# Features 256 to 639 of the first tokens: DMA transposes in place of TensorE turns

## The chip, the cores and the metric

The kernel runs on one core of a Trainium2 chip. A core has TensorE (matrix multiplication into PSUM), VectorE, ScalarE and GpSimd (elementwise work) and SyncE, which here only issues DMAs; each follows its own queue of instructions and waits for the others through semaphores. The metric is the time of one execution on the device in microseconds, the median of several runs. Data is bf16; PSUM holds f32.

## The reference

The input x holds 2048 tokens of 640 features. Two branches see the same x and a gate of each token mixes them:

```python
g = sigmoid((x * gate_w).sum(-1, keepdims=True))
# branch A: a state space layer with 640 complex states
dt = exp(log_dt); Lam_bar = exp(dt * Lam)
B_bar = ((Lam_bar - 1.0) / Lam)[:, None] * Bmat
Bu = einsum("bld,pd->blp", x, B_bar)
for t in range(L):                 # L = 2048
    h = Lam_bar * h + Bu[:, t, :]
a = 2.0 * einsum("blp,dp->bld", hseq, Cmat).real + x * Dskip
# branch B: a dense layer of two matrices, hidden size 1728
b = gelu(x @ w1 + b1) @ w2 + b2
return g * a + (1 - g) * b
```

## The kernel before, in words

**Tiling.** The tokens are cut into four chunks of 512 (c = 0 to 3), a chunk into four blocks of 128 tokens (a = 0 to 3), the 640 features into five slices of 128 (kd = 0 to 4), and the 1728 hidden columns into 14 groups (kf), 13 of 128 and one of 64. The first dense layer (`ff1`, `ff1_mm`, L264) and the product with B (`ssm`, L540) need x with the features on the partitions: the tile `xT[c]`, 128 partitions by 5 slices by 512 tokens. The skip term x * Dskip (`seed`, L576) needs x with the tokens on the partitions: the tile `xn[c]`. The second dense layer is `fin_b` (L605), the product of the states with C is `fin_a` (L653).

**Where xT comes from.** For chunks 1, 2 and 3 a DMA transpose reads x from DRAM and writes xT (L175, L184, L185). For chunk 0, x is loaded into `xn[0]`, block by block, and TensorE turns each block and slice by a matmul against an identity (`turn`, L232, with its matmul on L233). The result stands in PSUM, from where `turned` (L236) copies it to xT, with VectorE (L240) or ScalarE (L242). `turn_first` does this for slices 0 and 1 of a block, `turn_rest` for slices 2, 3 and 4, three matmuls and one copy of 384 columns a block. The constant KA = 2 marks the border between the two.

**The loads.** `load_x0` loads a part of `xn[0]`, `load_w1a` a slice of the first 768 columns of w1 (`w1a`, groups kf 0 to 5). The next 512 columns are `w1b`, the last 448 are `w1c`, with one more column that a copy fills with gate_w (L399). `rows` loads a parameter vector as rows of `prmA` (log_dt, Lambda_im, Lambda_re) or `prmB` (gate_w, b1), and a matmul against the identity turns these into columns (L371, L396). The loads stand at L138 to L186, nearly all in SyncE's queue; ScalarE's queue issues w1a[0], w1a[1] and one load of x0. SyncE issues in the order of the text. Semaphores are given to DMAs in turn, and a DMA that is given one already in use waits until the earlier DMA has landed.

**The order of work around the change.** From L188 on, the order of the instructions of TensorE, VectorE and ScalarE is the order of the text. After nine warming matmuls (L230), six banks of PSUM collect the groups kf 0 to 5 of chunk 0. `strip(kd, t0, t1, ...)` adds slice kd for tokens t0 to t1 to all six, and `part(kd, a)` is the strip of one block. Matmuls of slices 0 and 1 stand between the turns of the four blocks (L359 to L368), then come slices 2 and 4 and, with the last slice 3, the loop over kf at L394. Between them stand the small operations that make the step sizes, angles and decay (`dt16`, `dtl`, `thp_c`, `r_c`, `u`, `kk`, `red`, `ab`), the two sines on ScalarE (L391, L393), and the turned columns of prmB at kf = 3. Six GELUs follow on ScalarE, then w1b and w1c, then `ssm(0)`. While these run, VectorE doubles the tables of cosine and sine (L416 to L436), and then it scans.

**The later order** is written out at L686 to L710: ssm and ff1 of a chunk, and fin_b and fin_a some steps later. `let_out` and `dve_now` put VectorE's operations in between by planned times. Two buffers of `xn` are used in turn, so `load_xn(3)` (L701) stands after the last use of xn[1].

Of the kernel before, what the change touches and what calls it, by code (L numbers as in the profile page):

```python
# [12 lines left out]
BF16 = mybir.dt.bfloat16  # L13
# [3 lines left out]
P = 128  # L17
T = 2048
D = 640
F = 1728  # L20
CH = 512
NCH = T // CH
KD = D // P
KS = D // P
# [3 lines left out]
TPC = CH // P  # L28
H = TPC // 2
HT = H * P  # L30
# [11 lines left out]
def kernel(  # L42
# [19 lines left out]
    nc = tc.nc  # L62
    x2d = A_x.flatten_outer_dims()
# [3 lines left out]
    const = ctx.enter_context(tc.tile_pool(name="const", bufs=1))  # L67
# [7 lines left out]
    def bank(dtype=F32):  # L75
        return ps.tile([P, CH * 4 // (4 if dtype == F32 else 2)], dtype, name="bank")


    cut1 = FA * P
    FB = FA + 4  # L80
    cut2 = FB * P
    n1c = F - cut2 + 1
    xT = [const.tile([P, KD, CH], BF16, name=f"xT{c}") for c in range(NCH)]
    w1a = [const.tile([P, cut1], BF16, name=f"w1a_{kd}") for kd in range(3)]
    w1a34 = const.tile([P, 2, cut1], BF16, name="w1a34")
    w1a += [w1a34[:, j, :] for j in range(2)]
    w1b = [const.tile([P, cut2 - cut1], BF16, name=f"w1b_{kd}") for kd in range(KD)]
    w1c = [const.tile([P, n1c], BF16, name=f"w1c_{kd}") for kd in range(KD)]
    w2_sb = const.tile([P, KF - 1, D], BF16, name="w2_sb")
    BT_re, BT_im = ([const.tile([P, KD, n * P], BF16, name=f"BT_{ri}{n}") for n in (KSA, KS - KSA)] for ri in ("re", "im"))  # L90
    CT_re = const.tile([P, KS, D], BF16, name="CT_re")
# [4 lines left out]
    prmA = const.tile([P, P], BF16, name="prmA")  # L96
    NB = KS + KF - 1
    prmB = const.tile([P, P], BF16, name="prmB")
# [21 lines left out]
    def load_xn(c, a0=0, a1=TPC, queue=None):  # L120
        if a0 == 0:
            xn[c] = xnp.tile([P, TPC, D], BF16, name="xn")
        r0 = c * CH + a0 * P
        (queue or nc.sync).dma_start(out=xn[c][:, a0:a1, :], in_=x2d[r0:r0 + (a1 - a0) * P, :].rearrange("(a p) d -> p a d", p=P))

    def load_w1a(queue, kd):
        queue.dma_start(out=w1a[kd][:], in_=B_w1[kd * P:(kd + 1) * P, 0:cut1])

    def rows(queue, dst, v):
        queue.dma_start(out=dst, in_=v.rearrange("(j p) -> j p", p=P))  # L130

    KA = 2
    xn[0] = xnp.tile([P, TPC, D], BF16, name="xn")

    def load_x0(queue, a0, a1, d0, d1):
        queue.dma_start(out=xn[0][:, a0:a1, d0:d1], in_=x2d[a0 * P:a1 * P, d0:d1].rearrange("(a p) d -> p a d", p=P))
# [3 lines left out]
    load_x0(nc.sync, 1, 2, 0, KA * P)  # L140
    load_w1a(nc.scalar, 1)
    load_x0(nc.sync, 2, 3, 0, KA * P)
    load_x0(nc.scalar, 0, H, KA * P, D)
    load_x0(nc.sync, 3, 4, 0, KA * P)
    load_w1a(nc.sync, 2)
    nc.vector.memset(prmA[:], 0.0)
    nc.vector.memset(prmB[:], 0.0)
    warm = const.tile([P, 1], F32, name="warm")
    nc.scalar.activation(out=warm[:], in_=nc.const_aps.tensor(1.0, [P, 1], BF16), func=ACT.Exp)
    rows(nc.sync, prmA[0:KS, :], A_log_dt)  # L150
    rows(nc.sync, prmA[KS:2 * KS, :], A_Lambda_im)
    rows(nc.sync, prmA[2 * KS:3 * KS, :], A_Lambda_re)
    load_x0(nc.sync, H, TPC, KA * P, D)
    nc.sync.dma_start(out=w1a34[:], in_=B_w1[3 * P:KD * P, 0:cut1].rearrange("(k p) f -> p k f", p=P))
    rows(nc.sync, prmB[KS:NB, :], B_b1[0:(KF - 1) * P])
    rows(nc.sync, prmB[0:KS, :], gate_w)
    for kd in range(KD):
        nc.sync.dma_start(out=w1b[kd][:], in_=B_w1[kd * P:(kd + 1) * P, cut1:cut2])
    for kd in range(KD):
        nc.sync.dma_start(out=w1c[kd][:, 0:F - cut2], in_=B_w1[kd * P:(kd + 1) * P, cut2:F])  # L160
    make_identity(nc, ident[:])
    HC = CH // 8
    tfi = work.tile([P, HC], I32, name="e")
# [15 lines left out]
        nc.sync.dma_start(out=w2_sb[:, k0:k1, :], in_=B_w2[k0 * P:k1 * P, :].rearrange("(kf p) d -> p kf d", p=P))  # L179
    for h in range(2):  # L180
        nc.sync.dma_start(out=w2l[h * F_LAST:(h + 1) * F_LAST, :], in_=B_w2[(KF - 1) * P:F, :])
    nc.sync.dma_start(out=b2bc[:], in_=B_b2.rearrange("(o d) -> o d", o=1).to_broadcast([P, D]))
    nc.sync.dma_start(out=Dbc[:], in_=A_Dskip.rearrange("(o d) -> o d", o=1).to_broadcast([P, D]))
    nc.sync.dma_start_transpose(out=xT[2][:], in_=x2d[2 * CH:3 * CH, :])  # L184
# [32 lines left out]
    def pe(cols):  # L217
        ck.pe += cols / 2400.0 + 0.002
# [9 lines left out]
    pA = bank()  # L228
# [3 lines left out]
    def turn(p, col, a, kd):  # L232
        nc.tensor.matmul(p[:, col:col + P], lhsT=xn[0][:, a, kd * P:(kd + 1) * P], rhs=ident[:], start=True, stop=True,  # L233
                         skip_group_check=True)

    def turned(engine, p, col, a, k0, k1):  # L236
        dst = xT[0][:, k0:k1, a * P:(a + 1) * P]
        src = p[:, col:col + (k1 - k0) * P].rearrange("p (k t) -> p k t", t=P)
        if engine is nc.vector:
            nc.vector.tensor_copy(out=dst, in_=src)  # L240
        else:
            nc.scalar.activation(out=dst, in_=src, func=ACT.Identity)  # L242

    def turn_first(a, other):
        t = bank()
        turn(t, 0, a, 0)
        turned(nc.vector, t, 0, a, 0, 1)
        turn(other, a * P, a, 1)
        turned(nc.scalar, other, a * P, a, 1, 2)

    turn_first(0, pA)

    def col(name, dtype=F32, n=KS):
# [10 lines left out]
    def ff1_mm(p, c, kf, kd, t0=0, t1=CH, first=None, last=KD - 1):  # L264
        w, f0 = (w1a, 0) if kf < FA else (w1b, FA) if kf < FB else (w1c, FB)
        w = w[kd][:, (kf - f0) * P:(kf - f0 + 1) * P]
        nc.tensor.matmul(p[:, t0:t1], lhsT=w, rhs=xT[c][:, kd, t0:t1],  # L267
                         start=(kd == 0) if first is None else first, stop=(kd == last), skip_group_check=first is not None)
        pe(t1 - t0)
# [53 lines left out]
    banks = [bank() for _ in range(FA)]  # L323

    def strip(kd, t0, t1, first, f0=0, f1=FA):
        for kf in range(f0, f1):
            ff1_mm(banks[kf], 0, kf, kd, t0, t1, first, 3)

    def turn_rest(a, t, *parts):
        for k in range(KA, KD):  # L330
            turn(t, (k - KA) * P, a, k)
        for engine, k0, k1 in parts:
            turned(engine, t, (k0 - KA) * P, a, k0, k1)

    HB = CH // 2

    def scratch(i):
# [16 lines left out]
    def part(kd, a):  # L354
        strip(kd, a * P, (a + 1) * P, kd == 0)
# [10 lines left out]
    turn_first(3, pA)  # L366
    part(0, 2)
    part(1, 2)  # L368
    turn_rest(0, pA, (nc.scalar, KA, KD))
    pP = bank()  # L370
    nc.tensor.matmul(pP[:, 0:3 * KS], lhsT=prmA[:], rhs=ident[:, 0:3 * KS], start=True, stop=True, skip_group_check=True)  # L371
    nc.vector.tensor_copy(out=colA[:], in_=pP[:, 0:3 * KS])
    nc.scalar.activation(out=dt16[:], in_=ldt_c, func=ACT.Exp)
    nc.vector.tensor_scalar(out=limp[:], in0=lim_c, scalar1=INV_2PI, scalar2=None, op0=ALU.mult)
    part(0, 3)
    turn_rest(1, bank(), (nc.vector, KA, KD))
    nc.vector.tensor_tensor(out=dtl[:], in0=dt16[:], in1=lre_c, op=ALU.mult)
    nc.vector.tensor_tensor(out=thp_c[:], in0=dt16[:], in1=limp[:], op=ALU.mult)
    nc.scalar.activation(out=r_c[:], in_=dtl[:], func=ACT.Exp)
    nc.vector.tensor_tensor(out=u, in0=tf[:].rearrange("p (o i) -> p o i", o=1).to_broadcast([P, KS, NP]), in1=over(thp_c[:], NP), op=ALU.mult)  # L380
    part(1, 3)
    part(2, 0)
    part(2, 1)
    turn_rest(2, pA, (nc.scalar, KA, KD))
    turn_rest(3, bank(), (nc.vector, KA, KD))
    nc.vector.tensor_copy(out=kk[:], in_=u)
    nc.vector.tensor_tensor(out=red, in0=u, in1=kk[:], op=ALU.subtract)
    strip(KD - 1, 0, HT, False)
    part(2, 2)
    part(2, 3)  # L390
    nc.scalar.activation(out=FSC[:, 0:KS, 0:NP], in_=red, func=ACT.Sin, scale=TWO_PI_M)  # L391
    nc.vector.scalar_tensor_tensor(out=ab, in0=red, scalar=-1.0, in1=red, op0=ALU.mult, op1=ALU.max)
    nc.scalar.activation(out=FSC[:, KS:2 * KS, 0:NP], in_=ab, func=ACT.Sin, scale=-TWO_PI_M, bias=halfpi[:])  # L393
    for kf in range(FA):  # L394
        if kf == 3:
            nc.tensor.matmul(pA[:, 0:NB], lhsT=prmB[:], rhs=ident[:, 0:NB], start=True, stop=True, skip_group_check=True)  # L396
            nc.vector.tensor_copy(out=colB[:], in_=pA[:, 0:NB])
            for j in range(KD):
                nc.vector.tensor_copy(out=w1c[j][:, n1c - 1:n1c], in_=pA[:, j:j + 1])  # L399
        for kd in (4, 3):  # L400
            ff1_mm(banks[kf], 0, kf, kd, HT if kd == 4 else 0, CH, False, 3)
    for kf in range(FA):
        ff1_act(banks[kf], 0, kf)
    two_banks = [bank(), bank()]
# [24 lines left out]
    for ks in range(KS):  # L429
        for dst, X, xs, Y in ((TCOS, FS, nsH, FC), (TSIN, FC, sH, FS)):  # L430
            t = work.tile([P, HB], F32, name="g")
# [108 lines left out]
    def ssm(c, at={}):  # L540
        hs[c] = hsp.tile([P, 2 * KS, CH], BF16, name="hs")
        for ks in range(KS):
            if ks in at:
                at[ks]()
            bu = work.tile([P, 2, CH], BF16, name="bu", bufs=8)
            for ri, BT in enumerate((BT_re, BT_im)):
                p = bank()
                for kd in range(KD):
                    nc.tensor.matmul(p[:], lhsT=BT[ks >= KSA][:, kd, (ks % KSA if ks < KSA else ks - KSA) * P:][:, 0:P], rhs=xT[c][:, kd, :],  # L549
                                     start=(kd == 0), stop=(kd == KD - 1))  # L550
                    pe(CH)
                nc.scalar.activation(out=bu[:, ri, :], in_=p[:], func=ACT.Identity)  # L552
                act(0.6)
            scan_ops(c, ks, bu, ck.act)
            if c == 0 and ks == 0:
                later(0, 1.6, factors)
            let_out(ck.pe)
# [140 lines left out]
    ssm(2, {KS - 1: lambda: first_banks(1)})  # L698
    fin_b(1, seeds(1))
    fin_a(1)  # L700
    load_xn(3)  # L701
    ssm(3)
    gel_tile(3)
    ff1(3, 0, {KF - 3: lambda: first_banks(2)})
# [36 lines left out]
```

## Time and profile before

| | |
|---|---|
| median of three runs | 215.61 us (215.58 to 215.92) |
| the profiled execution, its own time | 215.9 us |
| its span, first to last instruction | 214.1 us |
| TensorE busy | 210.6 us, 98% of the span |
| VectorE, ScalarE busy | 189.1 us (88%), 102.7 us (48%) |
| granted TensorE clock | 1.000 |
| DMA moved | 15.84 MB |

The profile is one execution. The span runs from the first to the last instruction; the rest of the execution's own time lies around it. Busy time counts the instructions of an engine, not its waits. A TensorE matmul's end is modelled, so a wait of TensorE is better seen in the distance between the starts of two matmuls. The chain of work goes back from the last instruction to whatever released it, step by step. A DMA is shown twice: by the time that its queue took to issue it, and by the time from its issue to its landing. PE is TensorE, DVE is VectorE, ACT is ScalarE, and SPq and ACTq are the DMA queues of SyncE and ScalarE.

### The profile page before, as it was taken

The page shows a single profiled execution, that of the slowest core. Times are in us where ns is not written, and L with a number is a line of the kernel's source. Part 1 is how long each engine was busy: PE and PEld are TensorE (multiplying, and loading weights), DVE is VectorE, ACT ScalarE, POOL GpSimd, SP SyncE. Part 2 cuts the span into 40 slices and gives each one's busy share as a digit, 9 for nine tenths or more (in the row PEclk, how much of TensorE's full clock was granted, in tenths as well). Part 3 has the DMA queues.
Part 4 walks back from the last instruction along what each step waited for, and adds up shares of the span by engine and source line. Part 5 has one row for each costly group of instructions (what it writes and reads, how often), then busy time and mean ns, then how long its engine had stood idle before and what let it go on. Part 6 is the DMA issues. An engine that isn't in the chain of part 4 may idle for free.

```text
span 214.1 us, 3607 instructions
## 1 busy us (share of the span) xinstructions
PE 210.6 (98%) x1413; PEld 127.4 (59%) x1413; DVE 189.1 (88%) x387; ACT 102.7 (48%) x185; POOL 1.0 (0%) x13
## 2 busy tenths in 40 slices
PE   8999999999999999999999999999999999999994
PEld 5955444454475644775457777444457687676773
DVE  1589999999998999999999999999999999993153
ACT  3499856675759579203573210455683422305100
POOL 1000000000000000000000000000000000000000
PEclk9999999999999999999999999999999999999999
DMA  6869999999000000042000005100000000100011
GB/s 191 232 147 202 207 183 287 324 211 186 0 0 0 3 0 0 17 136 109 0 3 0 0 0 183 65 0 2 3 0 14 3 0 31 61 34 0 0 66 61
DMA packets 31571, 15.84 MB, mean 74 GB/s; under 512 B 22978, under 2 KB 31554, under 8 KB 31554
## 3 DMA queue, kind: packets, MB, share of 16 engines
q1 hardware_dynamic: 30850, 14.99, 29.2%
q10 hardware_dynamic: 704, 0.62, 0.9%
q8 instruction: 11, 0.18, 0.3%
q14 instruction: 6, 0.05, 0.1%
HBM read 7.48 MB, written 2.62 MB: 47 GB/s over the span
## 4 chain that ended last, share of the span: by engine, by line
PE 98%; DVE 0%; issue 0%
PE bank L267 27%; PE bank L608 27%; PE bank L667 20%; PE bank L549 20%; PE bank L230 1%; PE bank L624 1%; PE bank L293 1%; PE bank L233 1%; DVE ot L672 0%; PE bank L358 0%; PE bank L283 0%; PE bank L396 0%; PE bank L371 0%
## 5 line engine op out<-in xcount | busy, mean ns | idle before, releaser
L608 PE MATMUL bank<-w_sb,gel 128*128 128x384 bf16 (+1 forms) x416 | 57.9, 299 | 0.0
L608 PEld LDWEIGHTS <-gel 128*128 128x128 bf16 x416 | 40.3, 98 | 17.0 <-issue 0.8
L552 ACT ACTIVATE bu<-bank 128x512 bf16<-128x512 f32 x40 | 23.6, 597 | 37.3 <-PE bank L549 37.3
L272 ACT ACTIVATE gel<-bank,colB 128x512 bf16<-128x512 f32 x52 | 33.7, 693 | 10.4 <-PE bank L267 10.1
L667 PEld LDWEIGHTS <-hs 128*128 128x128 bf16 x330 | 31.7, 98 | 11.6
L503 DVE TENSOR_TENSOR_SCAN g<-r_c,carry,v 128x512 bf16<-128x512 f32 x30 | 37.2, 1268 | 0.0
L616 ACT ACTIVATE gb<-bank,gcol 128x384 f32<-128x384 f32 (+1 forms) x32 | 15.1, 526 | 32.9 <-PE bank L608 16.4
L267 PE MATMUL bank<-xT,w1a 128*128 128x512 bf16 (+2 forms) x180 | 28.6, 315 | 0.0
L667 PE MATMUL bank<-CT_re,hs 128*128 128x320 bf16 (+2 forms) x165 | 27.1, 295 | 0.0
L667 PE MATMUL bank<-CT_im,hs 128*128 128x320 bf16 (+2 forms) x165 | 27.1, 295 | 0.0
L672 DVE SCALAR_TENSOR_TENSOR ot<-bank,gcol,gb 128x320 bf16<-128x320 f32 (+2 forms) x33 | 17.4, 531 | 9.6 <-PE bank L667 8.2
L549 PE MATMUL bank<-xT,BT_re 128*128 128x512 bf16 x100 | 24.8, 379 | 0.0
L549 PE MATMUL bank<-xT,BT_im 128*128 128x512 bf16 x100 | 24.8, 379 | 0.0
L267 PEld LDWEIGHTS <-w1a 128*128 128x128 bf16 x180 | 15.5, 102 | 11.3
L267 PE MATMUL bank<-xT,w1b 128*128 128x512 bf16 x80 | 17.9, 379 | 0.0
L549 PEld LDWEIGHTS <-BT_im 128*128 128x128 bf16 x100 | 9.8, 98 | 11.8
L582 DVE TENSOR_TENSOR bank<-xn,Dbc 128x320 f32<-128x320 bf16 (+2 forms) x33 | 14.5, 480 | 2.1 <-ACT gb L616 2.1
L549 PEld LDWEIGHTS <-BT_re 128*128 128x128 bf16 x100 | 9.6, 98 | 11.0
L484 DVE TENSOR_TENSOR v<-wa,wb 128x512 bf16<-128x512 bf16 x40 | 15.2, 421 | 0.6
L597 ACT ACTIVATE bank<-b2bc 128x384 f32<-128x384 bf16 (+1 forms) x24 | 11.7, 529 | 7.6 <-DVE ot L672 7.6
L484 DVE TENSOR_TENSOR wa<-TCOS,g 128x1024 bf16<-128x1024 bf16 x20 | 13.7, 684 | 0.1
L267 PE MATMUL bank<-xT,w1c 128*128 128x512 bf16 x60 | 13.7, 379 | 0.0
(99 smaller groups left out, 166.1 us busy)
## 6 DMA issues: line engine op xcount, KB each, us to landing
out_dram<-ot SPq DMA_DIRECT2D x15, 160.0 KB, 1.8
w_sb<-in_B_w_dram SPq DMA_DIRECT2D x1, 2080.0 KB
xn<-in_A_x_dram SPq DMA_DIRECT2D x3, 640.0 KB
w1b<-in_B_w_dram SPq DMA_DIRECT2D x5, 128.0 KB, 3.6
w1c<-in_B_w_dram SPq DMA_DIRECT2D x5, 112.0 KB, 3.2
w1a<-in_B_w_dram ACTq DMA_DIRECT2D x2, 192.0 KB, 3.0
w1a<-in_B_w_dram SPq DMA_DIRECT2D x1, 384.0 KB, 3.7
xn<-in_A_x_dram SPq DMA_DIRECT2D x4, 64.0 KB, 3.6
```

The source lines that it names most:

```text
L267: nc.tensor.matmul(p[:, t0:t1], lhsT=w, rhs=xT[c][:, kd, t0:t1], start=(kd == 0) if first is None else first, stop=(kd == last), skip_grou ...
L272: nc.scalar.activation(out=gel[c][:, kf, :], in_=p[:, :], func=ACT.Gelu_apprx_tanh, bias=b1_c[:, kf:kf + 1])
L484: nc.vector.tensor_tensor(out=o, in0=a, in1=b, op=op)
L503: nc.vector.tensor_tensor_scan(s["g"][:, ri, :], r_c[:, ks:ks + 1].to_broadcast([P, CH]), s["v"][:, ri, :], init, ALU.mult, ALU.add)
L549: nc.tensor.matmul(p[:], lhsT=BT[ks >= KSA][:, kd, (ks % KSA if ks < KSA else ks - KSA) * P:][:, 0:P], rhs=xT[c][:, kd, :], start=(kd == 0 ...
L552: nc.scalar.activation(out=bu[:, ri, :], in_=p[:], func=ACT.Identity)
L582: dve_now(ck.pe, 0.45, lambda: nc.vector.tensor_tensor(out=p[:, 0:d1 - d0], in0=xn[c][:, a, d0:d1], in1=Dbc[:, d0:d1], op=ALU.mult))
L597: nc.scalar.activation(out=v, in_=src, func=ACT.Identity)
L608: nc.tensor.matmul(p[:, col:col + d1 - d0], lhsT=gel[c][:, kf, a * P:(a + 1) * P], rhs=w2_sb[:, kf, d0:d1], start=False, stop=False, skip_ ...
L616: nc.scalar.activation(out=gbs[ti][:, d0:d1], in_=p[:, col:col + d1 - d0], func=ACT.Identity, scale=gcol[:, 1, ti:ti + 1])
L667: nc.tensor.matmul(p[:, 0:d1 - d0], lhsT=hs[c][:, j, lo:lo + P], rhs=CT[:, j % KS, d0:d1], start=False, stop=(j == 2 * KS - 1), skip_group ...
L672: nc.vector.scalar_tensor_tensor(out=ot[:, d0:d1], in0=p[:, 0:d1 - d0], scalar=gcol[:, 0, ti:ti + 1], in1=gbs[ti][:, d0:d1], op0=ALU.mult, ...
```

## The change

Slices 2, 3 and 4 (features 256 to 639) of chunk 0 no longer come from TensorE. Two DMA transposes in SyncE's queue, each for two blocks (256 tokens by 384 features), write them to xT[0]. `turn_rest` is gone with its twelve matmuls and four copies. `xn[0]` needs the same features for the skip term only and gets them by one load behind w2. The strips of slices 2 and 4 are cut at other places. Beside that:

- log_dt, Lambda_im and Lambda_re are issued by ScalarE's queue;
- ScalarE's load of x0 and SyncE's second one are gone from the start;
- w1a[3] and w1a[4] are two loads, 4 ahead of 3, instead of one, and w1c is two loads instead of five;
- the second copy of block 0 is VectorE's instead of ScalarE's;
- xn[3] is loaded in two halves.

```diff
-    w1a = [const.tile([P, cut1], BF16, name=f"w1a_{kd}") for kd in range(3)]
-    w1a34 = const.tile([P, 2, cut1], BF16, name="w1a34")
-    w1a += [w1a34[:, j, :] for j in range(2)]
+    w1a = [const.tile([P, cut1], BF16, name=f"w1a_{kd}") for kd in range(KD)]
...
-    w1c = [const.tile([P, n1c], BF16, name=f"w1c_{kd}") for kd in range(KD)]
+    w1c_lo = const.tile([P, 3, n1c], BF16, name="w1c_lo")
+    w1c_hi = const.tile([P, 2, n1c], BF16, name="w1c_hi")
+    w1c = [w1c_lo[:, j, :] for j in range(3)] + [w1c_hi[:, j, :] for j in range(2)]
...
     load_x0(nc.sync, 2, 3, 0, KA * P)
-    load_x0(nc.scalar, 0, H, KA * P, D)
+    nc.vector.memset(prmA[:], 0.0)
+    nc.vector.memset(prmB[:], 0.0)
+    rows(nc.scalar, prmA[0:KS, :], A_log_dt)
     load_x0(nc.sync, 3, 4, 0, KA * P)
     load_w1a(nc.sync, 2)
-    nc.vector.memset(prmA[:], 0.0)
-    nc.vector.memset(prmB[:], 0.0)
...
-    rows(nc.sync, prmA[0:KS, :], A_log_dt)
-    rows(nc.sync, prmA[KS:2 * KS, :], A_Lambda_im)
-    rows(nc.sync, prmA[2 * KS:3 * KS, :], A_Lambda_re)
-    load_x0(nc.sync, H, TPC, KA * P, D)
-    nc.sync.dma_start(out=w1a34[:], in_=B_w1[3 * P:KD * P, 0:cut1].rearrange("(k p) f -> p k f", p=P))
+    for a in range(0, TPC, H):
+        nc.sync.dma_start_transpose(out=xT[0][:, KA:KD, a * P:(a + H) * P], in_=x2d[a * P:(a + H) * P, KA * P:D])
+    rows(nc.scalar, prmA[KS:2 * KS, :], A_Lambda_im)
+    rows(nc.scalar, prmA[2 * KS:3 * KS, :], A_Lambda_re)
+    load_w1a(nc.sync, 4)
+    load_w1a(nc.sync, 3)
...
-    for kd in range(KD):
-        nc.sync.dma_start(out=w1c[kd][:, 0:F - cut2], in_=B_w1[kd * P:(kd + 1) * P, cut2:F])
+    for t, k0, k1 in ((w1c_lo, 0, 3), (w1c_hi, 3, KD)):
+        nc.sync.dma_start(out=t[:, :, 0:F - cut2], in_=B_w1[k0 * P:k1 * P, cut2:F].rearrange("(k p) f -> p k f", p=P))
...
         nc.sync.dma_start(out=w2l[h * F_LAST:(h + 1) * F_LAST, :], in_=B_w2[(KF - 1) * P:F, :])
+    load_x0(nc.sync, 0, TPC, KA * P, D)
...
-        turned(nc.scalar, other, a * P, a, 1, 2)
+        turned(nc.scalar if a else nc.vector, other, a * P, a, 1, 2)
...
-    turn_rest(0, pA, (nc.scalar, KA, KD))
...
     part(0, 3)
-    turn_rest(1, bank(), (nc.vector, KA, KD))
...
     part(1, 3)
-    part(2, 0)
-    part(2, 1)
-    turn_rest(2, pA, (nc.scalar, KA, KD))
-    turn_rest(3, bank(), (nc.vector, KA, KD))
+    strip(2, 0, HT, False)
     nc.vector.tensor_copy(out=kk[:], in_=u)
     nc.vector.tensor_tensor(out=red, in0=u, in1=kk[:], op=ALU.subtract)
-    strip(KD - 1, 0, HT, False)
-    part(2, 2)
-    part(2, 3)
+    strip(2, HT, CH, False)
+    strip(4, 0, CH, False)
...
-        for kd in (4, 3):
-            ff1_mm(banks[kf], 0, kf, kd, HT if kd == 4 else 0, CH, False, 3)
+        ff1_mm(banks[kf], 0, kf, 3, 0, CH, False, 3)
...
-    load_xn(3)
+    load_xn(3, 0, H)
+    load_xn(3, H, TPC)
```

More of the change, by code (lines that the diff above doesn't have):

```diff
@@ L327, in strip @@
             ff1_mm(banks[kf], 0, kf, kd, t0, t1, first, 3)
[L329 to L333, printed above, removed]
     HB = CH // 2
```

## The prediction

> **What bounds the kernel.** I read the page first: how busy each engine is, and the chain of work that ended last.
>
> ```profile
> span 214.1 us, 3607 instructions
> ...
> PE 210.6 (98%) x1413; PEld 127.4 (59%) x1413; DVE 189.1 (88%) x387; ACT 102.7 (48%) x185; POOL 1.0 (0%) x13
> ...
> PE 98%; DVE 0%; issue 0%
> ```
>
> The end is set by TensorE alone: the chain runs through its matmuls from 0.77 us to the last store, and no other engine holds 1% of it. Whatever shortens TensorE's queue ends the kernel earlier, as long as nothing makes TensorE wait instead. So I read the same chain in order of time where the change works (start us, us, what):
>
> ```profile
> 7.39 0.17 PE bank L233 x3
> 7.56 0.01 PE bank L371
> 7.57 0.35 PE bank L267 x6
> 7.92 0.27 PE bank L233 x3
> 8.19 1.14 PE bank L267 x18
> 9.33 0.34 PE bank L233 x6
> 9.66 2.30 PE bank L267 x24
> ```
>
> The L233 pieces are the twelve turns (3, 3 and 6). At these places 128-column matmuls start every 0.056 us, so twelve are worth 0.67 us; they hold 0.78 because the fourth waited 0.10 us (a start 0.157 after the one before it) for a bank that VectorE was still reading. The 18 matmuls at 8.19 should take 18 x 0.056 = 1.00 and take 1.14: the 13th waits 0.14 us for VectorE's 0.56 us copy (L240) of a turned block.
>
> Then what DMA does meanwhile: the DMA list (issue to landing, us), SyncE's waits, and the windows (last figures: DMA share, GB/s).
>
> ```profile
> xT<-in_A_x_dram SPq DMA_TRANSPOSE x3, 5.9
> BT_re<-in_A_B_re_dram SPq DMA_TRANSPOSE x2, 5.2
> BT_im<-in_A_B_im_dram SPq DMA_TRANSPOSE x2, 5.3
> ```
>
> ```profile
> SPq L130 <- DMA w1a<-in_B_w_dram: 0.4, 1, 0.4
> SPq L154 <- DMA xn<-in_A_x_dram: 0.3, 1, 0.3
> ```
>
> ```profile
> 4.00:5.00 1.00, 1.00 (x12) 1.00 (x11) 0.29 (x1) 0.29 (x2) 0.00 (x0) 1.00 1.05 322
> 5.00:6.00 1.00, 1.00 (x12) 1.00 (x11) 0.23 (x1) 0.12 (x1) 0.00 (x0) 1.00 0.58 146
> ...
> 16.00:22.00 6.00, 6.00 (x47) 3.12 (x46) 5.79 (x11) 5.99 (x13) 0.00 (x0) 1.00 1.16 199
> ```
>
> Transposes take over 5 us to land here, though they are larger (256x640 and 512x640) than the new ones. SyncE's waits show a limit: each DMA of the load block reuses the semaphore of the DMA eight places before it and isn't issued until that has landed. The DMA engines are full from 2 to 5 us and half idle from 5 to 6.
>
> [...] the trace agrees (0.107 us until 5.9 us, 0.056 after), so the turns are all in the cheap stretch. [...] the four 320 KB B transposes land at 18.03, 20.11, 22.04 and 23.97 us (semaphore records), about 2.0 us each or 164 GB/s, so I use 2.0. [...]
>
> **The change part by part.**
>
> Twelve turns leave TensorE: 12 x 0.056 = 0.67. The bank wait and the copy wait were made by turned blocks, so they go too: 0.10 + 0.14. Strips of 256 and 512 columns (0.109 and 0.216 us) replace pairs of narrower matmuls: 24 x 0.056 = 1.34 becomes 12 x 0.109 = 1.31, and 12 x 0.109 becomes 6 x 0.216, 0.01 less. The gain on the chain is 0.95 us if all data is there.
>
> Two copies leave VectorE (0.56 each) and two ScalarE (0.49 each); one 128x128 copy (0.28 to 0.29) moves to VectorE, which ends it near 4.2, before TensorE reads it at 4.67. None of these is on the chain. The dependent work must follow, and does: without the copies VectorE's dtl moves from 8.70 to about 8.0, the sine from 11.3 to about 10, and the first GELU waits only for the b1 column, 0.9 earlier with TensorE. VectorE has the least cover later: it writes the last pieces of the first chunk's hs at 86.1 and 86.4, and TensorE reads them from 87.3 and 88.0. A TensorE 0.95 us earlier still finds them, and VectorE's own chain starts earlier too (its colB copy waits for TensorE's L396).
>
> The first x columns of the four blocks keep their loads. The 192 KB load on ScalarE's queue and its twin on SyncE's (384 KB) leave the start and come back as one load behind w2, near 33 us: about 1.3 us more in front of b2bc, the turned x of chunks 2 and 3, xn and the first gelL transpose. gelL lands at 53.6 and is read at 64.5; b2bc lands at 43.2 and is used near 55. Hidden.
>
> The parameter rows now go through ScalarE's queue. log_dt is issued at 1.66 in the place of the load. Lambda_im and Lambda_re wait for the third and fourth DMAs (landed 3.85 and 4.15), so ScalarE issues them by 4.5 at 0.3 each, before its first turned block is ready at 4.70. They took up to 2.9 us to land on SyncE's queue, so 7.2 at worst; TensorE wants them at 7.23. Taken: no wait.
>
> Transposes: SyncE ends the w1a load at 3.02. The first transpose is about the ninth to eleventh DMA, so it waits for a landing between 3.4 and 4.15: issued 3.5 to 4.2. Issue costs 1.45 us for ten 128x128 blocks (BT_re), 0.9 for six, so the second goes at 4.4 to 5.1. The first B transpose moved its first packet 1.3 us after issue: 5.0 to 5.4, when the w1a data ahead has drained. Time to landing, bounded: gelL (two blocks, SBUF to SBUF) took 2.3 from issue, BT_re 4.74 with nothing transposing ahead. Six blocks on the line between give 3.5; landing 7.0 to 7.7. The second follows by 6/10 of 2.0 = 1.2: 8.2 to 8.9. Low bound for both 2.3 from issue, high bound 5.2.
>
> TensorE wants the first at 7.93 (7.40 - 0.17 for the first three turns, 0.03 for L371, 12 x 0.056), the second 6 x 0.109 later at 8.58, w1a[4] at 9.24, w1a[3] 6 x 0.216 later at 10.5, prmB at 11.2. w1a[4] is issued near 6 and lands about 0.4 behind the second transpose, 9.0; w1a[3] 0.6 later. So the second transpose is the one at the edge: I take 8.6 with half a microsecond either way: between no stall and 0.5, and 0.2 as the value. Both ends stay for the range: none, or 10.2 - 8.6 = 1.6.
>
> Behind them: the first w1b load now waits for the first transpose's landing and the second for the second's, so w1b is issued at 7.7 to 10.7 instead of 6.7 to 9.0. TensorE reads w1b[0] from 11.9 and w1b[4] from 13.6, and loads take about 3 us: cover at least 1.0 us. w1c in two DMAs instead of five saves three issues of 0.43 us, so the B transposes are issued no later than before (13.3); their first read is at 21.05 with 3.0 us to spare. The split load of xn[3] adds one issue of 0.6 us near 134 us, 50 us before its use.
>
> Sum: 214.1 - 0.95 + 0.2 = 213.35 of span. The profiled execution took 215.9 in all, 1.8 around its span, and the median is 215.61. Against the median: 215.6 - 0.75, about **214.9 us**.
>
> **Rivals.**
> - A, on time: the second transpose lands by 9.0, and the stall is at most 0.4. 214.5 to 215.1. The half-idle DMA stretch at 5 to 6 us speaks for it.
> - B, somewhat late: it lands at 9.0 to 10.0, or w1a[4] behind it at 9.6 to 10.6. The stall takes 0.4 to 1.4 and the time is 215.0 to 216.0, mostly no change.
> - C, late, the slower side: a transpose takes 5.2 us whatever its size. Issued at 5.0, the second lands at 10.2 or later, TensorE stands 1.6 us or more at the second strip, and all weights behind it are late as well: 216.1 to 217. It decides from a landing at 10.0 (8.58 + 0.95 + 0.43), since each microsecond there costs one. For it: the fixed-looking 5.2 and 5.3; against it: 2.3 for gelL, and that these rows include queueing behind the transpose before.
> - D, ScalarE's queue: if the two rows get the slots of later loads (5.2 to 6.3 us), ScalarE stands in front of its second turned block, TensorE waits for it near 5.5 and for the rows at 7.2: 215.5 to 217. The order of issue before gives no sign of it.
> - E, the turns go but the time comes back at hs near 86 us: 215.6. Against it: the cover worked out above.
>
> **Chances.** A 0.58, B 0.18, C 0.14, D 0.06, E 0.04. Faster by over 0.2% (0.43 us, about what can be told from no change here): A and a third of B, 0.64. Within: most of the rest of B, and E, 0.15. Slower: C, D and the tail of B, 0.21. The likeliest case's own range is 214.5 to 215.1; to hold 8 in 10 the range goes up through B to the edge of C, 214.5 to 216.1.
>
> **What would show it.** Right: L233 eight times only, none after 6.7 us, TensorE's first w1b matmul near 11.9 to 12.1 (12.80 before), the rest of the chain shifted by the same amount. Late transposes: a start-to-start gap over 0.11 us at the first matmul on w1a[2] with 256 columns, or on w1a[4]. D: ScalarE's second L242 later than 4.7. E: w1b near 12 but the L667 group of chunk 0 at its old 86.98. I would be wrong mostly through the landing time of a 256x384 transpose, which no row here shows.

## The result: slower, by what the merged w1c tiles do

| | before | after |
|---|---|---|
| median | 215.60 us (215.09 to 215.92, four runs) | 220.82 us (220.55 to 221.81, four runs) |
| the profiled execution's own time | 215.9 us | 221.1 us |
| its span | 214.1 us | 219.3 us |
| first matmul on w1b starts | 12.80 us | 12.12 us |
| second matmul on w1b starts | 13.02 us | 16.50 us |
| last matmul ends | 211.35 us | 216.53 us |

The ratio of after to before is 1.0253, with the 95% interval [1.0214, 1.0292]. The forecast was 214.9 us; it was wrong in sign, and 220.82 us lies outside its range. In after every line number has moved: the first dense layer's matmul is L269, the copies of the gate columns are L389, the transposes L151.

The page of after still shows TensorE at 96% of the span. It is the chain that differs: 7% of it is now DMA and SyncE's queue, and the row of the granted clock has one slice that isn't full (the fourth, which begins at 16.4 us).

```profile
span 219.3 us, 3528 instructions
...
PE 211.2 (96%) x1372; PEld 126.3 (58%) x1383; DVE 188.6 (86%) x386; ACT 102.7 (47%) x182; POOL 1.0 (0%) x13
...
PEclk9996999999999999999999999999999999999999
...
PE 91%; DMA 4%; SPq 3%; issue 1%; DVE 0%
```

The chain of after in order of time (start us, us, what) says where it leaves TensorE. Before 16.5 us it doesn't run through TensorE's matmuls, but through SyncE's issues of the two transposes and of the weights behind them, up to the second w1c load:

```profile
3.62 1.33 SPq L151
5.00 1.27 SPq L151
...
10.52 0.43 SPq L161
...
10.99 5.20 DMA w1c_hi<-in_B_w_dram
...
16.21 0.24 DVE w1c_hi L389 x2
...
16.50 7.04 PE bank L269 x24
```

What releases that chain is five copies of one column. In the kernel before, VectorE's timeline (start us, us, engine, line, operation, tiles; in brackets the idle time ahead and what ended it) has them straight behind the copy of the parameter columns:

```profile
12.10 0.18 DVE L397 COPY colB<-bank 128x18 f32<-128x18 f32 x1 [0.49 <-PE bank L396]
12.20 0.41 DVE L399 CAST w1c<-bank 128x1 bf16<-128x1 f32 x5
```

The same view of after:

```profile
11.68 0.18 DVE L387 COPY colB<-bank 128x18 f32<-128x18 f32 x1 [1.15 <-PE bank L386]
15.58 0.29 DVE L389 CAST w1c_lo<-bank 128x1 bf16<-128x1 f32 x3 [3.72 <-DMA w1c_lo<-in_B_w_dram]
16.21 0.23 DVE L389 CAST w1c_hi<-bank 128x1 bf16<-128x1 f32 x2 [0.34 <-DMA w1c_hi<-in_B_w_dram]
```

Each of these copies writes gate_w into the last column of a w1c slice. In before each slice is a tile of its own, the load fills the columns ahead of the last one, and the copy ran at 12.2 us while the five loads landed between 13.2 and 14.4: nothing waited. In after three slices share a tile, and two share another. The list of changes names the two loads; the two tiles stand only in the diff. The columns of all but a tile's last slice now lie between pieces that one load writes, and the copies wait until the whole load has landed, 15.56 and 16.19 us. No byte is written by both; that the order comes from the columns lying inside the load's range is an inference.

And TensorE waits for the copies, because they read the bank pA: six of the eight banks still hold groups, and the second of `two_banks` takes over pA's. TensorE's timeline of after shows one matmul on w1b into the other bank, and then nothing:

```profile
11.48 0.81 PE L269 MATMUL bank<-xT,w1a 128*128 128x512 bf16 x3
12.12 0.38 PE L269 MATMUL bank<-xT,w1b 128*128 128x512 bf16 x1
16.50 3.80 PE L269 MATMUL bank<-xT,w1b 128*128 128x512 bf16 x9 [4.00 <-DVE w1c_hi L389]
```

From the start at 12.12 to the one at 16.50 there are 4.38 us, where 0.216 is usual: 4.16 us are lost. In before the same place held twenty matmuls in one go (12.80 to 17.12).

The third part of the loss is in the windows of after (window, then busy us and instructions of PE, PEld, DVE, ACT and POOL, then the granted clock, DMA share, GB/s):

```profile
12.00:16.00 4.00, 0.50 (x3) 0.01 (x1) 0.29 (x3) 3.99 (x7) 0.00 (x0) 1.00 0.99 199
...
17.00:18.00 1.00, 1.00 (x4) 0.34 (x3) 0.96 (x3) 0.00 (x0) 0.00 (x0) 0.50 1.16 260
18.00:19.00 1.00, 1.00 (x3) 0.30 (x2) 0.96 (x3) 0.00 (x0) 0.00 (x0) 0.50 0.63 123
...
20.00:21.00 1.00, 1.00 (x6) 0.41 (x5) 1.00 (x2) 0.88 (x2) 0.00 (x0) 1.00 1.17 222
```

When TensorE restarts, its granted clock is 0.50 ("cold" below, "warm" being the full clock): 512-column matmuls start every 0.427 us until 19.9 us, then every 0.216 again. That costs 1.70 us over what those starts take warm. So: 0.68 gained up to the first w1b matmul, 4.16 lost to the wait, 1.70 lost to the cold clock, together +5.18 us. The last matmul ends 216.53 - 211.35 = 5.18 later, so the three terms are the whole.

### The profile page after: what moved, and what is told of

Same layout as the page of the kernel before. It is cut to its first block, busy times and chain, and to the rows that moved or that the text cites. A ratio compares the mean times of both kernels' runs of the same rounds, so it can differ in the third digit from the quotient of the medians.

```text
span 219.3 us, 3528 instructions
## 1 busy us (share of the span) xinstructions
PE 211.2 (96%) x1372; PEld 126.3 (58%) x1383; DVE 188.6 (86%) x386; ACT 102.7 (47%) x182; POOL 1.0 (0%) x13
## 3 DMA queue, kind: packets, MB, share of 16 engines
HBM read 7.48 MB, written 2.62 MB: 46 GB/s over the span
## 4 chain that ended last, share of the span: by engine, by line
PE 91%; DMA 4%; SPq 3%; issue 1%; DVE 0%
PE bank L597 26%; PE bank L269 23%; PE bank L656 20%; PE bank L538 20%; DMA w1c_hi<-in_B_w_dram 2%; DMA w1a<-in_B_w_dram 1%; SPq L151 1%; PE bank L613 1%; PE bank L295 1%; SPq L159 1%; SPq L127 0%; SPq L130 0%; SPq L161 0%; DVE ot L661 0%; DVE w1c_hi L389 0%
## 5 line engine op out<-in xcount | busy, mean ns | idle before, releaser
L274 ACT ACTIVATE gel<-bank,colB 128x512 bf16<-128x512 f32 x52 | 34.6, 686 | 17.1 <-PE bank L269 16.8
L269 PE MATMUL bank<-xT,w1a 128*128 128x512 bf16 (+2 forms) x158 | 27.8, 332 | 0.2
L269 PE MATMUL bank<-xT,w1b 128*128 128x512 bf16 x80 | 19.8, 405 | 4.0 <-DVE w1c_hi L389 4.0
L269 PEld LDWEIGHTS <-w1a 128*128 128x128 bf16 x162 | 14.7, 103 | 11.8
L269 PEld LDWEIGHTS <-w1b 128*128 128x128 bf16 x80 | 8.2, 103 | 15.0 <-DVE w1c_hi L389 4.5
```

What stands on the lines that cost most here:

```text
L274: nc.scalar.activation(out=gel[c][:, kf, :], in_=p[:, :], func=ACT.Gelu_apprx_tanh, bias=b1_c[:, kf:kf + 1])
```

## The experiments

All were timed beside the kernel before on the same chip (1 to 4, 5 to 8 and 9 apart, so that kernels of different groups compare by the ratio). "End" is the end of the last matmul in one profiled execution (before: 211.35). The timed runs of before alone reach from 214.94 to 216.56 us, so ends that differ by half a microsecond tell what happened in two executions, not what is usual.

| kernel | end us | span us | median us, and of before beside it | ratio, 95% interval |
|---|---|---|---|---|
| 1 after, w1c in five | 211.39 | 214.4 | 216.35, 215.93 | 1.0022 [1.0011, 1.0034] |
| 2 before, w1c in two | 213.21 | 216.1 | 218.94, 215.93 | 1.0158 [1.0104, 1.0212] |
| 3 after, gate columns by GpSimd | 211.74 | 214.5 | 216.42, 215.93 | 1.0026 [1.0015, 1.0037] |
| 4 after, the wait filled | 214.97 | 217.7 | 219.61, 215.93 | 1.0178 [1.0149, 1.0206] |
| 5 kernel 1, three ot buffers | 210.80 | 213.8 | 215.93, 215.89 | 1.0007 [0.9996, 1.0019] |
| 6 before, three ot buffers | 211.30 | 214.0 | 215.78, 215.89 | 0.9999 [0.9987, 1.0010] |
| 7 kernel 1, 30 small matmuls more | 210.84 | 213.9 | 215.82, 215.89 | 1.0012 [0.9996, 1.0028] |
| 8 kernel 5, w1b in two, rows read later | 210.46 | 213.2 | 215.36, 215.89 | 0.9987 [0.9974, 1.0000] |
| 9 before, rows on ScalarE's queue | 211.24 | 214.0 | 215.76, 215.91 | 0.9996 [0.9981, 1.0011] |

**Kernels 1 and 2: undo the merging alone, do it alone.** The first asks whether the rest of the change is worth anything; the second whether merging w1c hurts without the transposes. The edit of kernel 1 against after (kernel 2 has the same lines the other way round, in before):

```diff
-    w1c_lo = const.tile([P, 3, n1c], BF16, name="w1c_lo")
-    w1c_hi = const.tile([P, 2, n1c], BF16, name="w1c_hi")
-    w1c = [w1c_lo[:, j, :] for j in range(3)] + [w1c_hi[:, j, :] for j in range(2)]
+    w1c = [const.tile([P, n1c], BF16, name=f"w1c_{kd}") for kd in range(KD)]
...
-    for t, k0, k1 in ((w1c_lo, 0, 3), (w1c_hi, 3, KD)):
-        nc.sync.dma_start(out=t[:, :, 0:F - cut2], in_=B_w1[k0 * P:k1 * P, cut2:F].rearrange("(k p) f -> p k f", p=P))
+    for kd in range(KD):
+        nc.sync.dma_start(out=w1c[kd][:, 0:F - cut2], in_=B_w1[kd * P:(kd + 1) * P, cut2:F])
```

> The changed kernel with w1c in five tiles and five loads again, as before the change; all else of the change stays. Tile theory (the five gate_w column copies now wait for the merged loads of w1c, because those loads and the columns share a tile; TensorE waits behind them for the bank that they read, and its clock goes cold): VectorE copies the columns right after colB, near 11.9 us, no wait of TensorE at its second w1b matmul, and the gain of the transposes that the trace after already shows at its first w1b matmul (12.12 against 12.80) stays: 0.6 to 0.7 us under the kernel before, ratio 0.997. Rival (the transposes push w1b and w1c back in SyncE's queue, and TensorE waits for data): the w1c loads are issued later still, with five issues, and the time stays at 220 us or above, ratio 1.02 or more.

> The kernel before with w1c alone in two tiles and two loads, and nothing else of the change. Tile theory: the copies of the gate_w columns wait for the merged loads, which land near 14 us here since nothing delays their issue (9.0 and 9.5 us), so TensorE's second w1b matmul starts near 14.3 instead of 13.0: 1.3 us slower, or 2.5 to 3 if the clock goes cold as well; 217 to 218.5 us. Rival (the transposes are the cost): no wait appears, two issues instead of five help or do nothing, 215.3 to 215.8 us.

Kernel 1's TensorE reads w1b[0] at 12.20 and never stands for L387, its copies of the gate columns, which VectorE makes at once: its end is 5.14 us earlier than after's.

```profile
11.86 0.41 DVE L387 CAST w1c<-bank 128x1 bf16<-128x1 f32 x5
...
12.20 1.89 PE L267 MATMUL bank<-xT,w1b 128*128 128x512 bf16 x8
14.26 2.76 PE L267 MATMUL bank<-xT,w1b 128*128 128x512 bf16 x12 [0.17 <-DMA w1b<-in_B_w_dram]
```

Kernel 2, which keeps all twelve turns, has the wait of after in small. Its timeline of TensorE:

```profile
12.73 0.38 PE L269 MATMUL bank<-xT,w1b 128*128 128x512 bf16 x1
14.88 4.26 PE L269 MATMUL bank<-xT,w1b 128*128 128x512 bf16 x19 [1.77 <-DVE w1c_hi L401]
```

It loses 1.93 us there (2.149 from start to start), and its end is 1.86 later than before's. The wait is shorter than in after because the loads stand earlier in SyncE's queue (issued at 8.63 and 9.12, not at 10.52 and 10.99, with no transposes ahead) while TensorE comes later (12.73, not 12.12). So merging and transposes each add to the 4.16. The clock stayed warm in this profile (mean granted clock 1.000), 2.15 us lying between the two starts. The four timed runs took 217.93, 217.97, 219.91 and 221.07; the profiled one is the first. The mean granted clock on record is 1.000 and 0.998 for the two short ones and 0.990 and 0.991 for the two long ones, after's being 0.992 with its 3.4 us at half clock. So the two long ones probably had a cold stretch as well; no trace shows what they waited for, or how long.

So the merging is the cause, from both sides. Both edits change the tiles and the loads together; five loads into the two shared tiles, which would tell one from the other, were not run. But kernel 1 isn't faster than before either, though a ratio of 0.997 was expected of it: 0.6 us of gain at w1b are gone by the end. Kernels 5 to 7 follow that up.

**Kernel 3: keep the merged tiles, break the chain at the bank.** VectorE copies the five columns from PSUM to a small tile, and GpSimd copies them from there into w1c.

```diff
+            gw = const.tile([P, KD], F32, name="gw")
+            nc.vector.tensor_copy(out=gw[:], in_=pA[:, 0:KD])
             for j in range(KD):
-                nc.vector.tensor_copy(out=w1c[j][:, n1c - 1:n1c], in_=pA[:, j:j + 1])
+                nc.gpsimd.tensor_copy(out=w1c[j][:, n1c - 1:n1c], in_=gw[:, j:j + 1])
```

> The changed kernel with its merged w1c; VectorE copies the five gate columns from PSUM into a small tile of its own at once, and GpSimd copies them from there into w1c. Tile theory: GpSimd waits for the loads of w1c in place of VectorE, the bank is free near 12 us, TensorE doesn't wait, and the time is that of the first of these kernels, 214.9 us within 0.2. Rival: as slow as the changed kernel, 220 to 221 us.

The wait for the load is still there, on an engine that nobody needs then. Its timeline, with TensorE, VectorE and GpSimd:

```profile
11.96 0.15 DVE L389 COPY gw<-bank 128x5 f32<-128x5 f32 x1
...
12.30 4.60 PE L269 MATMUL bank<-xT,w1b 128*128 128x512 bf16 x20
...
15.14 1.69 POOL L391 CAST w1c_lo<-gw 128x1 bf16<-128x1 f32 x3 [13.54 <-DMA w1c_lo<-in_B_w_dram]
```

All twenty w1b matmuls run in one go. So it isn't the load's lateness as such that costs 4 us: it is the reading of a PSUM bank that TensorE needs, in an instruction that also waits for a load. The time is that of kernel 1 (1.0026 and 1.0022), and not the 214.9 us expected.

**Kernel 4: the same wait, but TensorE kept busy.** Nineteen matmuls of constants into the first of the two banks fill the time until the copies; their result is overwritten. It asks what the cold clock costs by itself.

```diff
     two_banks = [bank(), bank()]
+    for _ in range(19):
+        nc.tensor.matmul(two_banks[0][:, 0:512], lhsT=ones(P), rhs=ones(512), start=True, stop=True)
```

> The changed kernel with 19 matmuls of 512 columns on constants put in ahead of the first w1b matmul, 19 x 0.216 = 4.1 us of work without use that writes the same bank as the first w1b group and is overwritten by it. If 1.7 of the 5.2 us are TensorE's cold clock after 4 us of standing still (eight starts 0.427 us apart instead of 0.216), the fill keeps it warm and the kernel is 1.5 to 1.8 us faster than the changed one: 219.0 to 219.3 us. If the clock isn't part of it, the time stays at 220.8 or rises.

The windows of this kernel where after's clock was halved:

```profile
17.00:18.00 1.00, 1.00 (x7) 0.47 (x5) 0.93 (x3) 0.00 (x0) 0.00 (x0) 1.00 0.83 185
18.00:19.00 1.00, 1.00 (x6) 0.42 (x5) 0.96 (x3) 0.44 (x1) 0.00 (x0) 1.00 0.76 124
```

Full clock, six or seven matmuls a microsecond where after had three or four. The end is 1.56 us earlier than after's (216.53 - 214.97): the cold clock, shown apart from the wait. The 1.70 read in the trace of after agrees: this kernel starts all twenty w1b matmuls at 16.41, after nineteen at 16.50, and 1.70 + 0.08 - 0.22 = 1.56. Nineteen useless matmuls brought the ratio to before from 1.0253 down to 1.0178. By the medians the gain is 1.21 us, a little short of the 1.5 to 1.8 expected.

**Why kernel 1 gains nothing.** Its page looks like another kernel's:

```profile
span 214.4 us, 3543 instructions
...
DVE 70%; PE 22%; DMA 4%; issue 2%; ACT 1%; DVEq 0%
```

The chain now runs through VectorE, the second bound that the prediction named. Kernel 1's waits (engine, line, what it waited for: us in total, times, longest) show what held it:

```profile
DVE ot L659 <- DMA out_dram<-ot: 1.6, 2, 0.9
...
PE bank L364 <- issue: 0.9, 1, 0.9
...
PE bank L267 <- DMA w1b<-in_B_w_dram: 0.2, 1, 0.2
```

VectorE, at 98.63 and 136.03, waits 0.93 and 0.70 us for a store of results to free one of two `ot` buffers. At 174.53 and 180.02 TensorE then stands 0.24 + 0.06 us for VectorE's seed (L569). With 0.33 at w1b[4] (14.26), that is 0.63, and the gain up to w1b is 0.60: the end moves by +0.04.

In before VectorE waits for no store in these stretches. Why here? The DMA records of the stretch from 94 to 99 us hold a queue for instructions, which carries packets of 16 KB. In kernel 1:

```profile
q8 instruction: 1, 0.02, 1.2%
...
out_dram<-ot SPq DMA_DIRECT2D x2, 160.0 KB, 3.7
```

The same stretch of before holds no such packet, and this:

```profile
out_dram<-ot SPq DMA_DIRECT2D x2, 160.0 KB, 1.8
```

The 3.7 and the 1.8 are not the same store: the view times only the stores whose landing it can pair, in kernel 1 the first of the two, in before the second. By the semaphore records the first took 3.66 us in kernel 1 and 2.42 in before, 1.2 us less.

One packet took 0.88 to 1.43 us of one of the 16 DMA engines in before and after; that a store (or load) in flight then has a share waiting behind it is a reading. Three of the eleven packets start at 10.13, 90.44 and 128.60 us in before, at 12.19, 96.34 and 133.76 in kernel 1. Each of kernel 1's three lies in the flight of a DMA that came late: w1b[4], landing at 14.21, and the stores issued at 94.87 and 131.87. Before has a late store too, at another place: issued at 203.79, 3.88 us, with a packet at 205.50, and VectorE waits 1.32 us for it when little is left to do. Kernels 5, 6 and 7 put the reading to the test.

**Kernels 5 and 6: a third ot buffer,** in kernel 1 and in before.

```diff
-            ot = fwork.tile([P, D], BF16, name="ot", bufs=2)
+            ot = fwork.tile([P, D], BF16, name="ot", bufs=3)
```

> The changed kernel with w1c in five tiles, and three buffers of ot instead of two. The kernel with five w1c tiles alone is 0.2% slower than before although TensorE is 0.26 us ahead at 167 us: there VectorE waits 0.93 and 0.70 us (98.6 and 136.0 us) for the output DMA that last read its ot buffer, and TensorE waits 0.24 us for VectorE's seed at 174.5. Theory (VectorE is the second bound, and the late output DMAs are what sets it back): with a third buffer both waits of VectorE go, and the wait of TensorE at 174.5 too; 0.2 to 0.7 us faster than with two buffers, ratio to before 0.999 within 0.0015. Rival (the lost gain lies at the front alone, in the wait for prmA): nothing changes, ratio 1.002.

> The kernel before with three buffers of ot, the counterpart. In its trace VectorE waits for an output DMA only once, after the last chunk is under way (1.3 us at 207.8), and TensorE never waits for it. Theory: no change within 0.1%, ratio 1.000. If it gains as much as the changed kernel does, the third buffer has nothing to do with the change.

In kernel 5 both waits of VectorE and the waits of TensorE at 174.5 and 180.0 are gone, though the stores are as late as in kernel 1, and the end is 0.55 us earlier than before's. In before the third buffer changes nothing. Only 0.30 of the 0.60 us between kernels 1 and 5 are the buffer's: the 0.33 at w1b[4] are gone too, because that load landed at 12.93 in this execution, with a packet at 11.70. By the median kernel 5 is level with before, where kernel 1 is 0.2% above it; the two intervals just overlap.

**Kernel 7: put the instructions back, not the work.** Thirty matmuls of 16 columns on constants, results unused, stand ahead of the matmul that turns the parameter rows (L366 here): TensorE's program is again as long as before's, and ot keeps two buffers.

```diff
     pP = bank()
+    for _ in range(30):
+        nc.tensor.matmul(pP[:, 0:16], lhsT=ones(P), rhs=ones(16), start=True, stop=True, skip_group_check=True)
```

> The changed kernel with w1c in five tiles, and 30 matmuls of 16 columns without use ahead of the matmul on prmA, where TensorE stands for about 1 us in that kernel; they are overwritten, and give TensorE's queue its 60 instructions back. Fetch theory: the DMA trace shows packets of 16384 B on a queue of kind instruction, 11 in an execution, each taking one DMA engine for 0.9 to 1.4 us; with fewer TensorE instructions they move from 10.1, 90.4 and 128.6 us to 12.2, 96.3 and 133.8 us, into the last w1b load and two output DMAs that then land a microsecond later. With the count restored the packets go back to about 10, 90 and 128 us, w1b[4] lands near 13, VectorE doesn't wait for output DMAs at 98 and 136 us, and TensorE doesn't wait for it at 174.5. The time: 0.3 to 0.6 us under the kernel with five tiles where the clock is warm early, less where it isn't. Rival (the output DMAs are late through the loads of xn next to them): the packets move but VectorE's waits stay.

The packets start at 9.76, 89.79 and 128.29 us, near those of before. The DMA list of the stretch from 94 to 99 us has the first store (the one timed here) at

```profile
out_dram<-ot SPq DMA_DIRECT2D x2, 160.0 KB, 2.5
```

and VectorE waits for none of them; w1b[4] lands at 13.31 instead of 14.21, before it is read. With thirty matmuls more, this execution ends 0.55 us earlier than kernel 1's. The timed runs don't tell the two apart (1.0012 and 1.0022, with intervals that overlap), but over all kernels the first store agrees with the reading: with a packet in its flight it took 3.66 to 3.75 us (kernels 1, 3, 5 and 8), without one 2.42 to 2.58 (before, kernels 6, 7 and 9). For the store near 131 us the packet is not the whole: 4.07 to 4.59 in the first four, but 2.94 to 4.09 in the others. Nor is it for w1b[4], as kernel 5 shows. So the reading fits kernel 1's first late store; what delayed the other two DMAs is shown in part only.

**Kernel 8: the version that the readings suggest.** Kernel 5, with w1b in two loads (its tiles have no column that anyone else writes, so merging them creates no wait) and the matmul of the parameter rows behind two more parts, since kernel 1's TensorE stood 1.03 us for them. (Not shown: the two loads, and the two parts leaving their old places.)

```diff
-    w1b = [const.tile([P, cut2 - cut1], BF16, name=f"w1b_{kd}") for kd in range(KD)]
+    w1b_lo = const.tile([P, 3, cut2 - cut1], BF16, name="w1b_lo")
+    w1b_hi = const.tile([P, 2, cut2 - cut1], BF16, name="w1b_hi")
+    w1b = [w1b_lo[:, j, :] for j in range(3)] + [w1b_hi[:, j, :] for j in range(2)]
...
+    part(0, 3)
+    part(1, 3)
     pP = bank()
```

> The changed kernel with w1c in five tiles, three ot buffers, w1b in two loads (slices 0 to 2 and 3 to 4) instead of five, and the matmul on prmA after the two strips of block 3 instead of ahead of them. If what keeps the transposes from gaining is the wait for prmA (about 1.0 us where the clock is warm early), the late w1b[4] (0.1 to 0.3) and VectorE (0.2 to 0.7), then TensorE passes its first w1b matmul by 12.1, doesn't wait at w1b[4] nor at 174.5, and the kernel is 0.5 to 0.9 us faster than before: 0.996 to 0.998. If the front is held by the landing of the transposes and of w1a[4], at 7.7, 8.7 and 9.3 us, moving the prmA matmul gains nothing and the ratio is 0.998 to 1.000.

Its timeline of TensorE:

```profile
7.74 0.17 PE L368 MATMUL bank<-ident,prmA 128*128 128x15 bf16 x1
7.92 3.48 PE L269 MATMUL bank<-xT,w1a 128*128 128x256 bf16 x21
11.23 0.17 PE L386 MATMUL bank<-ident,prmB 128*128 128x18 bf16 x1
...
11.91 1.46 PE L269 MATMUL bank<-xT,w1b_lo 128*128 128x512 bf16 x6
```

w1b at 11.91, 0.89 earlier than before's, and the end is 0.89 earlier too: nothing is given back. By the medians it is 0.5 us faster; the ratio is 0.9987, short of the 0.996 to 0.998 expected, with an interval that touches 1. It is the best of all kernels here, by about what can be told from no change.

**Kernel 9: the rows alone.** What made the parameter rows late, ScalarE's queue or the transposes? (As in after, VectorE makes the second copy of block 0.)

```diff
-    load_x0(nc.scalar, 0, H, KA * P, D)
+    rows(nc.scalar, prmA[0:KS, :], A_log_dt)
     load_x0(nc.sync, 3, 4, 0, KA * P)
...
-    rows(nc.sync, prmA[0:KS, :], A_log_dt)
-    rows(nc.sync, prmA[KS:2 * KS, :], A_Lambda_im)
-    rows(nc.sync, prmA[2 * KS:3 * KS, :], A_Lambda_re)
+    load_x0(nc.sync, 0, H, KA * P, D)
...
+    rows(nc.scalar, prmA[KS:2 * KS, :], A_Lambda_im)
+    rows(nc.scalar, prmA[2 * KS:3 * KS, :], A_Lambda_re)
```

> The kernel before with the second part of the change alone: the three parameter rows on ScalarE's queue, the twelve turns kept, and ScalarE's load of x columns moved to SyncE's queue beside its twin. It asks what made Lambda_re late in most kernels with the new transposes (landed 7.1 to 7.65 us; 6.0 to 6.8 in those without). If the transposes in flight hold it back: here it lands by 6.5 us, TensorE doesn't wait at the matmul that turns the parameter rows, and the time is within 0.3 us of before, 215.5 to 216.0. If ScalarE's queue itself makes it late: it lands at 7.1 to 7.6 here too. TensorE reaches that matmul near 7.7 to 8.0 with the turns kept, so the time is the same in both cases, unless the x columns, now later, hold up the first turns: then a wait of 0.3 to 1 us before the turn of a third x column block at 7.4 us, and 216 to 216.7.

Lambda_re is issued at 4.18 and has landed at 6.04 us, and TensorE turns the rows at 7.28 without a wait (earlier than the 7.7 to 8.0 expected: its clock was warm from 5.7 us, with 128-column matmuls starting every 0.056 us). So ScalarE's queue alone didn't make the row late here. With the transposes in flight, Lambda_re landed at 7.23 in after and at 7.49 in kernel 1, but at 6.23 in kernel 5: 1.19, 1.45 and 0.19 us later than here. That the transposes held it back is a reading; what decides it stays open.

## Why the prediction was wrong

**The step that failed** is "w1c in two DMAs instead of five saves three issues of 0.43 us". The merging was costed as a saving on SyncE's queue and as nothing else. The saving came (the first B transpose is issued at 12.04 us, 13.29 before). That two slices or three in one tile join a load and a copy that had nothing to do with each other was not looked at, nor who else uses the w1c tiles (the line of the gate columns stands in the code three lines above the last strip), nor which bank that copy reads. Kernel 2 has the cost alone: 1.93 us; in after it is 4.16, and 1.70 for the clock. None of the rivals A to E holds this case. C and D come to slower times, but through late transposes and ScalarE's slots, and neither happened.

**The transposes were right.** Landing was put at 7.0 to 7.7 and 8.2 to 8.9 us, between 2.3 and 5.2 from issue. Issued at 3.62 and 5.00, they landed at 7.48 and 8.21 (over all seven kernels with them, 7.35 to 8.01 and 8.11 to 8.74). The tile's answer for after, of the two new transposes:

```profile
L151 SPq DMA_TRANSPOSE xT<-in_A_x_dram x2: 1267/1301/1335, 3.6 to 5.0; - x2
...
DMA to landing us min/median/max: 3.2/3.5/3.9
```

The median of 3.5 is the value taken. The second landing has luck in it, since two errors cancel. The issue took 1.3 us, where 0.9 was estimated from BT_re's 1.45 by the number of blocks; gelL's issue, in the trace of before, takes 1.17 for two blocks, so in these three it hardly fell with them (1.45, 1.3, 1.17). And the second landed 0.73 behind the first, not 1.2. That 1.2 came from a misreading: only two of the four B transposes are of 320 KB, the other two being of 480 KB (384 rows). The second of 320 KB landed 2.08 us behind the first, those of 480 KB 1.93 behind the one ahead: 158 and 254 GB/s, not 164 throughout, so scaling 2.0 us by the blocks had no ground.

**The gain was nearly right, its parts less so.** 0.95 without stalls minus 0.2 was forecast up to w1b, 0.68 came. But there was no stall: from the parameter rows on, after's matmuls follow each other to w1b[0] with no distance over their own (one record is missing). TensorE read the rows at 7.50 and not at 7.23. About 0.19 of that 0.27 is the clock, which became warm (128-column matmuls starting 0.056 us apart and not 0.107; the clock column of the windows reads 1.00 on both sides) at 6.38 us and not at 6.00, and 0.08 the first turn, whose x landed at 3.41 and not at 3.22 (half of the 0.18 us, as it fell into the cold stretch). Over all kernels profiled the clock became warm between 4.0 and 6.4 us. What sets the moment, and whether the change bears on it, is not shown: the four without the new transposes (before, kernels 2, 6 and 9) lie at 5.7 to 6.0, six of the seven with them at 4.0 to 5.2. An earlier warm clock didn't help kernels 1 and 5: kernel 1 was warm at 4.5 us, stood 1.03 us for the rows, and reached w1b at 12.20; kernel 5 was warm at 4.0, waited 0.06, 0.28 and 0.64 for the transposes and w1a[4], and reached it at 12.24. There the data set the time: w1a[4], put at 9.0, landed at 9.45 in after and at 9.57 in kernel 5. That it would land about 0.4 us behind the second transpose was an estimate with no measurement behind it; in after it landed 1.24 behind (8.21 and 9.45). So after's having no stall is luck as well: at the forecast's pace it would have wanted w1a[4] at 9.24 and waited about 0.2 us (an estimate from these numbers).

**"Taken: no wait" for the rows** held in after: Lambda_re landed at 7.23, where 7.2 was called the worst, and was read at 7.50; with before's clock it would have been wanted at 7.23, just in time. In kernel 1 it cost 1.03 us. D was wrong in its mechanism: ScalarE issued both rows by 4.6 us.

**"Cover at least 1.0 us" for w1b[4]** was too much. It landed at 14.21 in kernel 1, 0.33 late, with an instruction packet in its flight; at 13.31 in kernel 7 without one. In after w1b[3] landed at 14.26: without the wait for the copies TensorE would have wanted it near 13.4 (12.12 plus six times 0.216, an estimate), so after's own loads were late behind the wait that hid them.

**E was the right kind of fear in the wrong place.** VectorE as the second bound takes half of the gain back in kernel 1, but at 174.5 and 180.0 us and through two late stores, not at the first hs of chunk 0 near 86.

**What stays open.** The medians give back part of what the profiles gain: kernel 5's end is 0.55 us earlier than before's and its median level with it, kernel 8's 0.89 and 0.5. Part of this is which execution was profiled: before's took 215.9 us, which is the median of its runs beside kernels 5 and 8 (215.89); theirs took 215.59 and 214.99, 0.34 and 0.37 below their medians. Why executions of one kernel spread by 1 to 1.6 us stays open. The moment at which the clock becomes warm may be part of it; one profile of a kernel can't show that.

## What to carry to other kernels

Before loads are merged into one tile, list every instruction that writes or reads any part of that tile, and what else each of them holds: here a one-column copy that had to wait for a load kept the PSUM bank that it reads, and TensorE behind it, until the load had landed (16.19 us; 4.16 us lost). If such a copy can't be avoided, take the data out of PSUM first and let an idle engine do the rest: in kernel 3 GpSimd then stood 13.54 us until the load had landed, and TensorE's twenty w1b matmuls ran in one go. A change that removes TensorE work should be judged by where the saved time surfaces next: here the front of the program was about 0.2 us from waiting for data (the estimate above, for after), and two waits of VectorE, 0.93 and 0.70 us, were enough for it to hold TensorE in kernel 1.

## What the runs showed of the hardware

- **The long wait cost twice.** After 4.38 us from one matmul to the next, in after, the next 3.4 us ran at a granted clock of 0.50, with 512-column matmuls 0.427 us apart and not 0.216 (1.70 us lost, 1.56 by kernel 4). After 2.15 us, in kernel 2's profile, the granted clock was 1.000. The clocks of 0.990 and 0.991 in two other runs of kernel 2 leave it open whether a wait shorter than 4.38 us can be enough.
- **Instruction packets of 16 KB stand among the DMA records**, eleven in before and eleven in after. The store of 160 KB near 95 us took 3.66 to 3.75 us with one in its flight (kernels 1, 3, 5 and 8) and 2.42 to 2.58 without (before, kernels 6, 7 and 9); for the one near 131 us the two ranges overlap (4.07 to 4.59, 2.94 to 4.09). That the packet is the cause is a reading. Between kernels 1 and 7, which differ by thirty small matmuls near 7 us, the three packets named above lie 2.43, 6.55 and 5.47 us apart, and the first store, issued at 94.87 in kernel 1, took 3.66 us there and 2.5 in kernel 7.
- **The issue of a transpose hardly shrank with its size:** 1.17 us for two blocks (gelL, before), 1.27 and 1.33 for six (after), 1.45 for ten (the first BT_re, before). The size is not all: the same BT_re took 2.71 in after.
